# A windowed attention with an MLP on one core: the float16 weighted sums of the last three chunks as two 64-query halves

## The chip, the cores and the metric

One core of one Trainium2 chip runs the kernel. The metric is device time in microseconds (us), from one launch; runs of the kernel before took 605.85, 604.10 and 605.22 us, median 605.22 us.

## The reference, cut to what matters

There are 4 batches, 8 heads, 768 positions and 64 values per head. Each query looks at itself and the 95 positions before it and at 8 global positions; all other scores are set so low that their weight is zero. The result of the attention goes through a two-layer MLP (512 to 2048 to 512) with a smooth activation.

```python
scores = scale * np.matmul(q, k.transpose(0, 1, 3, 2)) + bias      # bias falls with the distance
scores = np.where(keep, scores, -1000000000.0)
a = np.exp(scores - np.max(scores, axis=-1, keepdims=True))
a = a / (np.sum(a, axis=-1, keepdims=True) + 1e-09)
x = np.matmul(a, v)                                                # the weighted sums
h = x @ w_in
out = (h * np.tanh(softplus(h))) @ w_out
```

The change is in `np.matmul(a, v)`.

## The kernel before, in words

**Chunks and blocks.** The 3072 tokens are worked in 12 chunks of 256 queries (`ci` 0 to 11; three for each batch), each of two blocks of 128 queries (`blk`). Of a block's keys only a window is computed: 104 columns (96 earlier positions and 8 global ones) and the block's own 128. The first block of a batch has only its own 128 (`nk` is 1 there, 2 elsewhere; L401).

**Precision.** Chunks 0 to 2 (`CF32 = 3`) work in float32. From chunk 3 on each float32 operand is split into a float16 high part and a float16 low part, and a product is three float16 products: high by high, high by low, low by high.

**Attention, by steps.** A step `t` stands for two heads of one block, 8 steps per chunk; `where` and `shape` (L395 to L404) give its chunk, head group, block and pair of heads.
- `scores` (letter s, L418 to L438) multiplies queries and keys on TensorE, for two steps at a time. Its weights are 64 rows by 64 columns: head `j` uses 64 of the array's rows, each half of 64 queries 64 of its columns, so that four such products stand next to each other in program order.
- `largest` (t) takes the maximum on VectorE, `exps` (y) the exponential on ScalarE, `high_a` and `low_a` (g, p) split the result, and `turn_a` (X) transposes it by a DMA into the tile `AT`: keys on the partitions, 128 queries in the free dimension.
- `weigh` (W, L499 to L522) makes the weighted sums. For chunks 3 and later it takes the loop at L514: for each of two heads `j`, for each window part `kk` and each of the three precision terms, one product with `AT` as the weights (104 or 128 rows by 128 queries) and 64 columns of `v` streamed past them, accumulated in `pav[:, cols]`. That is 12 products a step, 6 in the first block of a batch. In chunks 0 to 2 the loop at L508 is used instead, whose weights are 64 columns of `v`, for two heads in turn.
- `rows` (R, L524) divides by the sums on VectorE, which reads `pav`; high_x, low_x and turn_x (T, U, V) prepare the MLP's input.

**MLP, by steps.** `moe_in` (i, L588, product at L597) makes 24 products of 128 by 128 weights with 256 columns; ScalarE, VectorE and GpSimd compute the activation; `moe_out` (o, L644, product at L656) makes 12 products with 512 columns (in the last chunk some of them with 256 or 128). `checks(1)` (L714) is one product near the end whose weights are 128 rows by 1 column, with 240 columns streamed.

**Order.** Every engine's order is written out by hand in `PROGRAM` (L739 to L796), a list of letters with numbers, and each engine takes its instructions in that order. Chunk 9 begins at step 72. TensorE's order around the steps W72 to W95 is below: each bracket is a run of weighted sums, with the TensorE steps just before and after it. There are 16 such runs.

```
i63 [W73] s78      o62 [W72] i65        i66 [W77 W76] i67   i68 [W75] s82
o67 [W74 W81] s84  s84 [W78 W79] o68    i71 [W82] s86       o71 [W85 W84] i72
i72 [W83 W80] i76  o72 [W87] o73        s92 [W86] i77       o76 [W88] i79
o78 [W89 W91] o79  o79 [W90] i81        o80 [W92 W93] i82   i82 [W94 W95] o81
```

Steps W72, W73, W76 and W77 have 6 products each, the other twenty 12: 264 products in all.

Of the kernel before, what the change touches and what calls it, by code (L numbers as in the profile page):

```python
# [20 lines left out]
P = 128  # L21
# [89 lines left out]
def windowed(st, tc, loc):  # L111


    nc = tc.nc
    L = NS()
    L.__dict__.update(loc)
    B, H, D, S, NB, NCC, NFB = L.B, L.H, L.D, L.S, L.NB, L.NCC, L.NFB
# [283 lines left out]
    def shape(t):  # L401
        ci, g, blk, a2 = where(t)
        first = ci % NCHB == 0 and blk == 0
        return ci, g, blk, a2, first, 1 if first else 2  # L404
# [94 lines left out]
    def weigh(t):  # L499
        ci, g, blk, a2, first, nk = shape(t)  # L500
        AT = pend.pop(t)
        if (ci, blk) not in pavs:
            pavs[ci, blk] = ps.tile([P, DM], F32, name=f"pav{blk}", bufs=1)
        pav = pavs[ci, blk]
        vs = [vown[ci][:, blk]] if nk == 1 else [vcmp[ci][:, blk], vown[ci][:, blk]]
        if ci < CF32:
            pair = slice((g * GH // 2 + a2) * P, (g * GH // 2 + a2 + 1) * P)
            for kk in range(nk):  # L508
                rows_ = slice(0, P if kk == nk - 1 else FB)
                for j in range(2):  # L510
                    h = g * GH + 2 * a2 + j
                    nc.tensor.matmul(pav[j * D:(j + 1) * D, pair], vs[kk][rows_, h * D:(h + 1) * D], AT[rows_, j * nk + kk, :], start=(kk == 0), stop=(kk == nk - 1))  # L512
            return
        for j in range(2):  # L514
            h = g * GH + 2 * a2 + j
            cols = slice(h * D, (h + 1) * D)
            n, last = 0, 3 * nk - 1
            for kk in range(nk):
                rows_ = slice(0, P if kk == nk - 1 else FB)
                for x, y in ((0, 0), (0, 1), (1, 0)):  # L520
                    nc.tensor.matmul(pav[:, cols], AT[rows_, (x * 2 + j) * nk + kk, :], vs[kk][rows_, y, cols], start=(n == 0), stop=(n == last))  # L521
                    n += 1  # L522

    def rows(n):  # L524
# [178 lines left out]
    def checks(i):  # L703
# [26 lines left out]
        "d": lambda p, other=False: low_k(p - 1, other), "N": units, "h": high_v, "l": low_v, "x": window_v,  # L730
        "e": begin, "K": lambda i: masks_far() if i else masks_own(), "L": mask_own, "M": mask_far,
        "s": scores, "t": largest, "y": exps, "g": high_a, "p": low_a, "X": turn_a, "W": weigh,
        "I": identity, "P": turn_p, "F": turned, "O": spread, "m": times_rb,
        "R": rows, "T": high_x, "U": low_x, "V": turn_x,
# [221 lines left out]
```

## Time and profile before

| | before |
|---|---|
| median of three runs | 605.22 us (604.10 to 605.85) |
| the profiled execution's own time | 605.78 us |
| its span, first to last instruction | 604.0 us |
| mean granted TensorE clock | 0.998 of full speed |
| TensorE products (PE) | busy 594.2 us, 98% of the span |
| weight loads (PEld) | busy 412.7 us, 68% |
| ScalarE, VectorE, GpSimd | 75%, 72%, 25% |

How to read the rows further down: PE is TensorE's products, PEld its weight loads, which run beside products. In a shape such as `104*128 104x64 f16` the part with the star is the weights (rows by columns) and the part with the x the streamed operand (rows by columns). L521 is line 521 of the kernel. A row of the timeline gives the start of the first instruction of a group, the time from there to the end of its last, the group, and how many there are. Products are pipelined and their ends are modelled: the duration of one is its latency, longer than the step from one start to the next. So the pace is read from starts, and the start of a group's last product is the row's start plus its length less the mean duration of one. DVE is VectorE, ACT ScalarE, POOL GpSimd.

### The profile page before, as it was taken

What the parts mean: (1) busy time and instruction counts of PE and PEld (TensorE: products, weight loads), DVE (VectorE), ACT (ScalarE), POOL (GpSimd) and SP (SyncE); (2) the same over time, 40 slices, a digit from 0 to 9 for tenths busy, and PEclk for the clock granted to TensorE, in tenths of its full rate; (3) what the DMA queues carried; (4) which work ended last, traced back from release to release, by engine and by line L of the source; (5) the groups of instructions that cost most, each with busy time, mean ns of one, the idle gap of its engine ahead of it and who ended that gap; (6) DMA issues with size and microseconds to landing.
All of it is one profiled execution on the core that took longest, in us unless ns stands there. A gap on an engine that the chain in (4) does not pass through costs nothing.

```text
span 604.0 us, 15002 instructions
## 1 busy us (share of the span) xinstructions
PE 594.2 (98%) x5775; PEld 412.7 (68%) x5775; DVE 437.5 (72%) x1188; ACT 454.2 (75%) x1130; POOL 150.5 (25%) x128
## 2 busy tenths in 40 slices
PE   7999999999999999999999999999999999999996
PEld 3678677785567676767667676767667766766784
DVE  7799989998978795684876767675786766462433
ACT  6899999989978777569676778677876864655652
POOL 0033321331040423123133422141242121301020
PEclk9999999999999999999999999999999999999999
DMA  8998674333294481634454453562345341310001
GB/s 206 274 290 309 218 178 131 102 91 75 76 203 110 66 210 36 162 102 109 69 144 115 131 129 84 162 130 60 101 70 142 68 119 36 89 36 1 35 2 37
DMA packets 123387, 71.14 MB, mean 118 GB/s; under 512 B 91792, under 2 KB 113168, under 8 KB 123312
## 3 DMA queue, kind: packets, MB, share of 16 engines
q1 hardware_dynamic: 122736, 69.88, 45.8%
q8 instruction: 46, 0.75, 0.5%
q10 hardware_dynamic: 576, 0.27, 0.3%
q14 instruction: 29, 0.24, 0.1%
HBM read 38.62 MB, written 6.29 MB: 74 GB/s over the span
## 4 chain that ended last, share of the span: by engine, by line
PE 92%; DMA 4%; ACT 2%; SPq 1%; DVE 0%; issue 0%; ACTq 0%; DVEq 0%
PE ph L597 41%; PE po L656 36%; PE pav L656 4%; PE pav L521 4%; PE sc L437 4%; DMA kr<-kd 2%; DMA vo<-v 2%; PE pav L512 1%; PE ph L490 1%; DMA AT<-hl 1%; PE ph L543 0%; ACT A L460 0%; ACT u L623 0%; ACT AT L148 0%; ACT u L627 0%
## 5 line engine op out<-in xcount | busy, mean ns | idle before, releaser
L597 PE MATMUL ph<-xT,wts 128*128 128x256 f16 x2304 | 263.6, 273 | 0.0
L597 PEld LDWEIGHTS <-wts 128*128 128x128 f16 x2304 | 223.1, 98 | 34.5 <-issue 0.4
L656 PE MATMUL po<-wts,gt 128*128 128x512 f16 (+1 forms) x1056 | 234.4, 374 | 0.0
L656 PEld LDWEIGHTS <-gt 128*128 128x128 f16 x1248 | 115.9, 98 | 118.3
L615 ACT ACTIVATE e<-ph 128x512 f32<-128x512 f32 x90 | 53.2, 591 | 95.5 <-PE ph L597 95.3
L152 POOL TENSOR_TENSOR gt<-gf,gt 128x512 f16<-128x512 f32 x50 | 61.9, 1240 | 229.6 <-DVE gt L146 155.2
L635 DVE CUSTOM_DVE_ANT_0 gf<-gf,u 128x512 f32<-128x512 f32 x96 | 72.3, 756 | 49.6 <-ACT u L627 47.7
L460 ACT ACTIVATE A<-A,nm 128x232 f32<-128x232 f32 (+1 forms) x192 | 88.2, 461 | 12.3 <-DVE nm L451 12.3
L631 DVE SCALAR_TENSOR_TENSOR gf<-e,ph 128x512 f32<-128x512 f32 x90 | 61.0, 682 | 49.1 <-ACT e L615 48.2
L152 POOL TENSOR_TENSOR hl<-A,hl 128x512 f16<-128x512 f32 (+1 forms) x43 | 50.3, 1180 | 110.3 <-ACT hl L148 43.5
L451 DVE CUSTOM_DVE_ANT_0 A<-sc,mb 128x232 f32<-128x232 f32 (+1 forms) x192 | 63.6, 374 | 12.7 <-PE sc L437 12.5
L627 ACT ACTIVATE u<-u 128x512 f32<-128x512 f32 x96 | 59.7, 624 | 1.9
L619 ACT ACTIVATE u<-e 128x512 f32<-128x512 f32 x96 | 59.8, 624 | 1.7
L623 ACT ACTIVATE u<-u 128x512 f32<-128x512 f32 x96 | 59.7, 623 | 1.6
L152 POOL TENSOR_TENSOR wts<-ws,wts 128x512 f16<-128x512 f32 x18 | 22.5, 1255 | 82.0 <-ACT wts L148 75.3
L152 DVE TENSOR_TENSOR gt<-gf,gt 128x512 f16<-128x512 f32 x46 | 34.3, 748 | 6.9 <-ACT gt L148 6.3
L460 ACT ACTIVATION_READ_ACCUMULATOR A<-A,nm 128x1 f32 x192 | 36.2, 188 | 0.0
L521 PEld LDWEIGHTS <-AT 128*128 128x128 f16 (+1 forms) x792 | 29.4, 97 | 7.2 <-DMA AT<-hl 0.8
L148 ACT ACTIVATE gt<-gf 128x512 f16<-128x512 f32 x39 | 24.3, 623 | 11.3 <-DVE gmax L635 9.2
L656 PE MATMUL pav<-wts,gt 128*128 128x512 f16 (+1 forms) x192 | 28.7, 299 | 0.0
L521 PE MATMUL pav<-vo,AT 128*128 128x64 f16 x432 | 28.0, 192 | 0.0
L146 DVE TENSOR_SCALAR gt<-gf 128x512 f16<-128x512 f32 x57 | 25.6, 452 | 1.5
(130 smaller groups left out, 563.8 us busy)
## 6 DMA issues: line engine op xcount, KB each, us to landing
wts<-w_in SPq DMA_DIRECT2D x12, 512.0 KB
wts<-w_out SPq DMA_DIRECT2D x12, 512.0 KB
qr<-qT SPq DMA_DIRECT2D x23, 256.0 KB
kr<-kd SPq DMA_DIRECT2D x32, 184.0 KB
out<-ob SPq DMA_DIRECT2D x23, 256.0 KB
vr<-v SPq DMA_DIRECT2D x9, 512.0 KB
vc<-vo SPq DMA_DIRECT2D x15, 192.0 KB
wr<-w_in SPq DMA_DIRECT2D x4, 512.0 KB
```

The lines of the kernel that those rows point to most:

```text
L152: (nc.vector if other else nc.gpsimd).tensor_tensor(out, in_, high, op=ALU.subtract)
L451: nc.vector.tensor_tensor_reduce(out=A[:, j, 0:w], in0=sc[j][:, 0:w], in1=m, scale=-1.0 / (UNIT if ci < CF32 else UNIT * SQ), scalar=3.0e3 ...
L460: nc.scalar.activation(A[:, j], A[:, j], AF.Exp, bias=nm[:, h:h + 1], scale=-1.0, accum_out=rs[:, h:h + 1])
L521: nc.tensor.matmul(pav[:, cols], AT[rows_, (x * 2 + j) * nk + kk, :], vs[kk][rows_, y, cols], start=(n == 0), stop=(n == last))
L597: nc.tensor.matmul(ph[:, j, :].rearrange("p (b t) -> p b t", b=2), wv4[:, 2 * fb, x, c * P:(c + 1) * P], xT[:, :, y * NCC + c, :], start=( ...
L615: nc.scalar.activation(mish[m]["e"], mish[m]["h"], AF.Exp, scale=-1.0 / (SV * SW), accum_out=esum[:, m:m + 1])
L619: nc.scalar.activation(u, mish[m]["e"], AF.Square, bias=0.5)
L623: nc.scalar.activation(mish[m]["r"], mish[m]["u"], AF.Ln, bias=0.25 / RS, scale=1.0 / RS)
L627: nc.scalar.activation(r, r, AF.Exp, scale=-1.0)
L631: nc.vector.scalar_tensor_tensor(gf, mish[m]["e"], 0.5, mish[m]["h"], op0=ALU.add, op1=ALU.mult)
L635: nc.vector.tensor_tensor_reduce(out=gf, in0=gf, in1=mish[m]["r"], scale=SG / (SV * SW * RS), scalar=0.0, op0=ALU.mult, op1=ALU.max, accum ...
L656: nc.tensor.matmul(pos[ci][t + k][:, cols], gt[:, x, j, t * P:(t + 1) * P], wv4[:, 2 * fb + 1, y, cols], start=(fb == 0 and n == 0), stop= ...
```

## The change

In `weigh`, for chunks 9, 10 and 11, each product with 128 columns of weights becomes two: one on the first 64 queries (columns of the array and partitions of `pav` 0 to 63), one on the other 64. Both stream the same 64 columns of `v`. The halves alternate in the innermost loop, so the two halves of one term follow each other. The start and stop flags of a term are given to both halves. The order of the steps and all else stay.

```diff
@@ -518,7 +518,8 @@
             for kk in range(nk):
                 rows_ = slice(0, P if kk == nk - 1 else FB)
                 for x, y in ((0, 0), (0, 1), (1, 0)):
-                    nc.tensor.matmul(pav[:, cols], AT[rows_, (x * 2 + j) * nk + kk, :], vs[kk][rows_, y, cols], start=(n == 0), stop=(n == last))
+                    for half in (slice(0, D), slice(D, P)) if ci >= 9 else (slice(0, P),):
+                        nc.tensor.matmul(pav[half, cols], AT[rows_, (x * 2 + j) * nk + kk, half], vs[kk][rows_, y, cols], start=(n == 0), stop=(n == last))
                     n += 1
```

## Rows read from the trace of the kernel before

**Rows 1.** The page: busy time by engine, and granted clock in 40 slices.
```profile
PE 594.2 (98%) x5775; PEld 412.7 (68%) x5775; DVE 437.5 (72%) x1188; ACT 454.2 (75%) x1130; POOL 150.5 (25%) x128
...
PEclk9999999999999999999999999999999999999999
```

**Rows 2.** The page: the chain that ended last, by engine and line.
```profile
PE 92%; DMA 4%; ACT 2%; SPq 1%; DVE 0%; issue 0%; ACTq 0%; DVEq 0%
```

**Rows 3.** Busy time in the stretch that holds steps W72 to W95.
```profile
core 0: us, PE busy (x) PEld busy (x) DVE busy (x) ACT busy (x) POOL busy (x), PEclk, DMA share, GB/s
409.00:532.00 123.00, 123.00 (x1243) 86.03 (x1241) 83.65 (x214) 87.10 (x223) 29.49 (x24) 1.00 0.37 86
```

**Rows 4.** Waits of PE over the whole span: total us, times, longest.
```profile
PE ph L318 <- DVE ws L314: 2.7, 1, 2.7
PE pav L512 <- DMA vo<-v: 1.0, 1, 1.0
PE pav L521 <- DMA AT<-hl: 0.3, 1, 0.3
```

**Rows 5.** PE groups by shape from 409 us on: busy us, mean ns of one.
```profile
L521 PE MATMUL pav<-vo,AT 128*128 128x64 f16 x144 | 9.3, 192 | 0.0
L521 PE MATMUL pav<-vc,AT 104*128 104x64 f16 x120 | 8.1, 192 | 0.0
L656 PE MATMUL pav<-wts,gt 128*128 128x128 f16 x96 | 6.7, 219 | 0.0
...
L437 PE MATMUL sc<-wc,ws 64*64 64x168 f16 x216 | 5.7, 237 | 0.0
```

**Rows 6.** Timeline of PE, two runs of 24 weighted-sum products and what follows them.
```profile
523.87 0.25 PE L521 MATMUL pav<-vc,AT 104*128 104x64 f16 x3
...
524.58 2.78 PE L597 MATMUL ph<-xT,wts 128*128 128x256 f16 x24
527.20 0.25 PE L521 MATMUL pav<-vc,AT 104*128 104x64 f16 x3
...
527.91 2.75 PE L656 MATMUL po<-wts,gt 128*128 128x512 f16 x12
```

**Rows 7.** Timeline of PE: weighted sums, the scores of one step, weighted sums.
```profile
447.30 0.25 PE L521 MATMUL pav<-vo,AT 128*128 128x64 f16 x3
447.48 0.63 PE L437 MATMUL sc<-wc,ws 64*64 64x168 f16 x24
448.05 0.26 PE L521 MATMUL pav<-vc,AT 104*128 104x64 f16 x3
448.14 0.25 PE L521 MATMUL pav<-vo,AT 128*128 128x64 f16 x3
```

**Rows 8.** Timeline of PE: float32 products with 64 columns of weights (L543).
```profile
15.56 0.44 PE L490 MATMUL po<-idn,A 128*128 128x128 f32 x2
15.93 1.09 PE L543 MATMUL ph<-idn,ri 128*64 128x128 f32 x16
16.95 0.66 PE L490 MATMUL po<-idn,A 128*128 128x128 f32 x4
```

**Rows 9.** Mean duration of these float32 products over the span.
```profile
L490 PE MATMUL po<-idn,A 128*128 128x128 f32 x56 | 9.7, 289 | 0.5 <-ACT A L460 0.3
...
L543 PE MATMUL ph<-idn,ri 128*64 128x128 f32 x96 | 6.5, 277 | 0.0
```

**Rows 10.** Timeline of PE around the one-column product L714.
```profile
595.15 0.83 PE L656 MATMUL pav<-wts,gt 128*128 128x128 f16 x12
595.92 0.26 PE L714 MATMUL sc<-ind,ones 128*1 128x240 f16 x1
596.11 2.12 PE L656 MATMUL po<-wts,gt 128*128 128x512 f16 x12
```

**Rows 11.** Timeline of PE: the scores of a batch's first block, then weighted sums.
```profile
243.90 0.53 PE L437 MATMUL sc<-wc,ws 64*64 64x64 f16 x24
244.36 0.26 PE L521 MATMUL pav<-vc,AT 104*128 104x64 f16 x3
```

**Rows 12.** The same scores by shape, those begun by 243.95 us: x is the count.
```profile
L437 PE MATMUL sc<-wc,ws 64*64 64x128 f16 x2 | 0.2, 240 | 0.0
L437 PE MATMUL sc<-wc,ws 64*64 64x64 f16 x3 | 0.2, 206 | 0.0
```

**Rows 13.** The same, those begun by 244.045 us.
```profile
L437 PE MATMUL sc<-wc,ws 64*64 64x128 f16 x6 | 0.4, 224 | 0.0
L437 PE MATMUL sc<-wc,ws 64*64 64x64 f16 x9 | 0.3, 197 | 0.0
```

**Rows 14.** Weight loads of the same scores begun by 243.92 us.
```profile
L437 PEld LDWEIGHTS <-ws 64*64 64x64 f16 x4 | 0.1, 103 | 0.2 <-issue 0.2
```

## The prediction, made before the changed kernel ran

> **What bounds the kernel now.** I read the page first. TensorE's products are busy 594.2 us of 604.0, no other engine over 75%, and the granted clock is full in every slice [rows 1]. Busy time alone doesn't prove a bound, so the next view is the chain that ended last: 92% of it is PE [rows 2]. Then the stretch in which the change acts, which the order of steps puts at 409 to 532 us: PE is busy all 123.00 us of it, at full clock, while ScalarE has 87.10 and VectorE 83.65 [rows 3]. The waits of PE confirm it: the only one that ever named the weighted sums is 0.3 us, once in the span, and the longest PE wait anywhere is a start-up one of 2.7 us [rows 4]. So in this stretch, and from there to PE's end, PE has no slack: what the change adds to PE's stream moves the end by as much, and what it saves there would be won in full. The producers of `AT` and the consumer of `pav` (VectorE at L535) have room on both sides; a PE that comes later only gives the first more time.
>
> Then the weighted sums themselves. The groups by shape have 144 and 120 products, 264 in all, as the order of steps says [rows 5]. Their mean of 192 ns is latency; the pace is in the starts. Two runs of 24 take 523.87 to 524.58 and 527.20 to 527.91, 0.71 us each [rows 6], so a product comes every 0.0296 us; the starts are rounded to 0.01, which leaves 0.0292 to 0.0300, and I take 0.0298. All 264 cost 7.9 us now. They stream 64 columns. A 128-column product comes every (0.83 - 0.219) / 11 = 0.0555 us [rows 5, 10], so 64 columns are worth 0.028 us. The pace is thus nearly that of the columns, and a half product still streams all 64 of them. **No column of time is removed**; the best the halves can do is to stand side by side and give the pace of before.
>
> **What is added.** (1) 264 products and 264 weight loads: a term is now two loads of 64 columns and two products. (2) Changes of the weights' width, 128 to 64 columns and back, around each run of weighted sums. (3) Nothing moves: DMAs, order, waits and other engines are the same. The second half's wait for `pav` or `AT` is met when the first's is, so I cost it at nothing; were it not met, PE would show it as a wait, of which there is now 0.3 us in all [rows 4].
>
> **The price of a change of width.** Four places show one.
> - From the weighted sums (128 columns of weights) to the scores (64 by 64): the last of three begins at 447.30 + 0.25 - 0.192 = 447.36, its columns take 0.03, the scores begin at 447.48: a hole of 0.09 us [rows 5, 7].
> - Back: the last score begins at 447.48 + 0.63 - 0.237 = 447.87, its 168 columns take 0.073, the next weighted sum begins at 448.05: 0.10 [rows 5, 7].
> - With all 128 rows in use and only the width changing, in float32: the last of L543 begins at 15.93 + 1.09 - 0.277 = 16.74. A round of its eight takes at most (1.09 - 0.277) / 7 = 0.116, and the next 128-wide one begins at 16.95: 0.09 or a little more [rows 8, 9].
> - In float16 with only the width changing, to a single column and back: the last 128-wide product begins at 595.15 + 0.61 = 595.76 and ends its columns at 595.82; L714 begins at 595.92, and its 240 columns (0.104 us) end at 596.02; the next begins at 596.11. The two holes together are 0.19 us [rows 5, 10].
> By contrast, weighted sums followed by a 128-wide MLP product leave no hole: 524.58 is the 24th step after 523.87 [rows 6]. So a change costs **0.095 us** in either direction, and it goes with the width alone. On top comes a first load that nothing covers. Into 64-wide weights: the first 64-column score begins at 243.90 and the third, the next of its tile, just before 243.95, 0.05 us where a later round takes 0.032 (below): 0.02 more [rows 11, 12]. Into 128-wide ones: the row at 448.05 is 0.26 long where its like is 0.25: 0.01 more [rows 7].
>
> **How many.** Of the 16 runs in the order of steps, 14 are entered from a 128-wide product and 12 left to one: 26 new changes. Two are entered from scores and four left to scores, where a hole stands already; the two entries cost the 0.01 us by which the first load is longer.
> 14 x 0.115 + 12 x 0.105 + 2 x 0.01 = **2.9 us**.
>
> **The pace inside a run.** No row has a float16 pair of column halves over all 128 rows, so I bound it. Below: the pace of before, 0.0298 a pair, since the columns set it. Above: two halves in turn, 2 x 0.0298, 0.06 a pair. The nearest row is the score tile with 64 columns of weights and 64 streamed: three had begun by 243.95, nine by 244.045; six more in two tiles are three rounds in 0.095 us, **0.0317** a round, with the other tiles running beside it [rows 12, 13]. I take 0.0317: 264 - 16 = 248 steps inside runs x 0.0019 = **0.5 us**. Why the halves should overlap: eight pairs of L543 are column halves over all 128 rows and take 0.116 us a pair, no more than the (0.66 - 0.289) / 3 = 0.124 of one full-width float32 product behind it, both with a first load in them [rows 8, 9]. Why the queue should keep up: 24 scores, loads included, begin within 0.53 - 0.22 = 0.31 us, 0.013 a product, where a half needs 0.016 [rows 11, 13].
>
> Here a page speaks against the change more than the rows do. The first four 64-wide loads begin within 0.02 us of each other, and a tile's load and product repeat every 0.0317 us [rows 13, 14]. The Trainium skill ("TensorE: Matmul & The Clock Gate", section "LDWEIGHTS (loading the stationary operand)") puts a load at its columns over 1.2 GHz, an estimate of 0.053 us for 64. By that a pair would take 0.053 and the sum would be 264 x 0.023 = 6.1 us instead of 0.5. The trace's 0.0317 disagrees, and I go by it.
>
> **The sum.** 2.9 + 0.5 = 3.4 us on PE, none of it covered. The profiled execution took 605.78 us (span 604.0 and 1.8 around it), which gives 609.2. That execution is 0.56 above the median of the runs, 605.22; against the median the forecast is **608.6**. About 0.3% of this kernel, 1.8 us, is what a measurement can tell from no change.
>
> **The rivals.**
> - *The halves load in turn.* Both column halves take their weights from the same 128 rows; if their loads queue, a pair takes two rounds of 0.0317, and 264 x (0.0634 - 0.0298) = 8.9 us come on top of 2.9: 617.0. For it: a load nearly fills the round already. Against it: the scores' loads, two of each four on the same 64 rows, start together [rows 14]. Chance 0.05. The load of 0.053 us that the page would have instead gives 605.2 + 2.9 + 6.1 = 614.2, in that case's tail.
> - *TensorE's queue is too slow.* Seven of the runs become 48 products at a stretch. No row shows more than 24 at a pace below 0.02 us. At the old pace a product, a pair takes 0.0596: 7.9 + 2.9 = 10.8, 616.0. Chance 0.04.
> - *Not slower: no hole between 128-wide and half-wide weights.* If TensorE emptied only where the rows change too, or for float32, the 26 holes would be absent. What is left is the pace and 14 first loads: 0.5 + 0.3 = 0.8 us, 606.0, no measurable change. It decides at the first MLP product behind a run: begins at once, or 0.1 us later. For it: L543 is float32 and L714 has one column, not 64. Against it: between them both doubts are met, and the hole was the same in all. Chance 0.06.
> - *Faster.* The pace would have to fall under that of the streamed columns, which no row shows; I leave 0.01 for it. That the change doesn't act can't be: the slices are explicit.
>
> **How the numbers follow.** The forecast has 0.84. Its own bounds: 26 x 0.09 with no first load and the old pace is 2.3, 607.5; holes and loads of 0.125 and a pace 0.005 slower are 3.3 + 1.2 = 4.5, 609.7. The runs shown scatter by 0.6 above and 1.1 below their median; a median scatters less, and I allow 0.6 to 0.7 on either side: 606.9 to 610.4. It leaves out the two slow rivals and the two others, 0.16. Slower by over 0.3%: 0.84 + 0.05 + 0.04 = 0.93. Within: 0.06. Faster: 0.01.
>
> **What would show it.** Right: 528 products at L521 with 64 columns of weights from chunk 9 on; a hole of about 0.1 us on either side of a run, as between i65 and W72; both halves of a term starting some ns apart, pairs 0.032 us apart, so that a run of 24 pairs takes 0.76 us where it took 0.71; the stretch from step i63 to o83 longer by 3.4 us, all else on PE as before; a clock still at full. Wrong: a pair every 0.05 us or more (loads or queue in turn), or MLP products that follow at once (no hole); a new wait of PE for `AT` or `gt`, or a clock that falls between the holes, would be causes not named here.

## The result and the profile after

The changed kernel took 609.08 us (median of four runs, 608.51 to 609.34) against 605.17 us for the kernel before (four runs, 604.10 to 605.85): a ratio of 1.0065, 95% interval 1.0051 to 1.0079. It is slower by 3.9 us; the forecast was 3.4 us more, 608.6.

The two profiled executions can be compared without the scatter of whole runs. The order of steps puts everything that the change touches between the first product of step i63 and the first of step o81, and TensorE never rests there. That stretch took 527.91 - 409.74 = 118.17 us before and 530.53 - 409.00 = 121.53 us after: **3.36 us**. From the start of o81 to the start of TensorE's last product it is 70.77 us before and 70.78 after. Ahead of the stretch, where the two programs are the same, i63 came 0.74 us earlier in the execution of after; behind TensorE's last product that execution took 0.6 us longer. These are the scatter that a whole run carries.

The busy time of the changed kernel's engines over just this stretch (columns as in [rows 3]):

```profile
core 0: us, PE busy (x) PEld busy (x) DVE busy (x) ACT busy (x) POOL busy (x), PEclk, DMA share, GB/s
...
408.99:530.53 121.54, 121.54 (x1478) 83.52 (x1476) 80.92 (x206) 83.13 (x217) 29.48 (x24) 1.00 0.37 86
```

PE is still busy all the time and at full clock; VectorE and ScalarE still have about 40 us to spare. A hole of 0.1 us doesn't show in this busy time, because each product is listed with a latency of 0.19 us or more that reaches across the hole; holes are read from starts. The groups of PE by shape, from 409 us on, against [rows 5]:

```profile
L522 PE MATMUL pav<-vo,AT 128*64 128x64 f16 x288 | 9.9, 196 | 0.0
L522 PE MATMUL pav<-vc,AT 104*64 104x64 f16 x240 | 8.8, 198 | 0.0
```

These are the 528 products with 64 columns of weights, twice 264. Now the timeline of PE around the last two runs, W92 W93 and W94 W95, to be laid beside [rows 6]:

```profile
523.36 2.75 PE L657 MATMUL po<-wts,gt 128*128 128x512 f16 x12
526.04 0.28 PE L522 MATMUL pav<-vc,AT 104*64 104x64 f16 x6
526.16 0.26 PE L522 MATMUL pav<-vo,AT 128*64 128x64 f16 x6
526.25 0.26 PE L522 MATMUL pav<-vc,AT 104*64 104x64 f16 x6
...
526.73 0.26 PE L522 MATMUL pav<-vo,AT 128*64 128x64 f16 x6
526.92 2.79 PE L598 MATMUL ph<-xT,wts 128*128 128x256 f16 x24
529.65 0.28 PE L522 MATMUL pav<-vc,AT 104*64 104x64 f16 x6
...
530.33 0.26 PE L522 MATMUL pav<-vo,AT 128*64 128x64 f16 x6
530.53 2.76 PE L657 MATMUL po<-wts,gt 128*128 128x512 f16 x12
```

All terms of the sum can be read here.
- **The hole on the way in.** The last of the twelve L657 products begins at 523.36 + 2.75 - 0.38 = 525.73, its 512 columns end at 525.95, the first half begins at 526.04: 0.09 us. Before, a weighted sum followed an MLP product without a hole: 527.20 is the 24th step after 524.58 [rows 6].
- **The first load.** The first row of a run lasts 526.04 to 526.16, 0.12 us for three terms, the later ones 0.095: 0.02 us that nothing covers.
- **The pace.** From 526.16 to 526.73 there are 18 terms: 0.0317 us for a pair of halves. A row of six products stands where one of three stood, and takes 0.095 instead of 0.089 us.
- **The hole on the way out.** The last row's three terms end at 526.73 + 0.095 = 526.82, the MLP begins at 526.92: 0.10 us. The MLP's own row is 2.79 long instead of 2.78, which the forecast puts down to a first load of 128 columns that nothing covers. The starts of the other runs show the same: 0.09 to 0.10 us at every one of the 26 new places.

One thing here goes beyond the forecast. Where a run lies beside scores, both sides now have weights of 64 columns, and only the rows differ (128 or 104 against 64). The timeline of PE after, a run that is left to scores and the next, which is entered from them:

```profile
447.48 0.26 PE L522 MATMUL pav<-vo,AT 128*64 128x64 f16 x6
447.67 0.63 PE L437 MATMUL sc<-wc,ws 64*64 64x168 f16 x24
448.23 0.28 PE L522 MATMUL pav<-vc,AT 104*64 104x64 f16 x6
```

The three terms of the first row end at 447.48 + 0.095 = 447.575, and the scores begin at 447.67: 0.095 us. The last score begins at 447.67 + 0.63 - 0.237 = 448.06, its columns end at 448.14, and the next run begins at 448.23: 0.09 us. So a change of the rows from 128 or 104 to 64, or back, makes the same hole with the width unchanged. The alternation of 104 and 128 rows inside a run makes none.

PE's waits show nothing new in the stretch (rows to be laid beside [rows 4], and one that is new; total us, times, longest):

```profile
PE ph L318 <- DVE ws L314: 2.7, 1, 2.7
PE pav L512 <- DMA vo<-v: 1.6, 1, 1.6
PE pav L522 <- DMA AT<-hl: 0.4, 1, 0.4
...
PE ph L598 <- DMA xT<-xhl: 0.3, 1, 0.3
```

Against [rows 4], the wait for a transposed tile is 0.4 us instead of 0.3, still once in the span. The new one is a wait of the MLP for its input. Both end ahead of the stretch, at 388 and 223 us, where the two programs are the same.

### The profile page after: what moved, and what is told of

Same layout as the page of the kernel before. It is cut to its first block, busy times and chain, and to the rows that moved or that the text cites. A ratio compares the mean times of both kernels' runs of the same rounds, so it can differ in the third digit from the quotient of the medians.

```text
span 607.2 us, 15530 instructions
## 1 busy us (share of the span) xinstructions
PE 596.1 (98%) x6039; PEld 412.4 (68%) x6039; DVE 437.9 (72%) x1188; ACT 454.1 (75%) x1130; POOL 150.6 (25%) x128
## 4 chain that ended last, share of the span: by engine, by line
PE 92%; DMA 4%; DVE 1%; ACT 1%; SPq 1%; issue 0%; DVEq 0%; ACTq 0%
PE ph L598 40%; PE po L657 35%; PE pav L657 4%; PE sc L437 4%; PE pav L522 4%; PE pav L512 2%; DMA vo<-v 1%; PE po L490 1%; PE ph L544 1%; DMA vc<-vo 1%; DMA xT<-xhl 1%; PE ph L490 1%; DMA AT<-hl 1%; DMA kr<-kd 1%; DVE A L451 0%
## 5 line engine op out<-in xcount | busy, mean ns | idle before, releaser
L657 PE MATMUL po<-wts,gt 128*128 128x512 f16 (+1 forms) x1056 | 234.4, 375 | 0.0
L657 PEld LDWEIGHTS <-gt 128*128 128x128 f16 x1248 | 115.7, 98 | 118.5 <-POOL gt L152 0.2
L522 PEld LDWEIGHTS <-AT 128*128 128x128 f16 (+3 forms) x1056 | 29.1, 104 | 9.9 <-issue 4.7
L657 PE MATMUL pav<-wts,gt 128*128 128x512 f16 (+1 forms) x192 | 28.7, 299 | 0.0
L522 PE MATMUL pav<-vo,AT 128*128 128x64 f16 (+1 forms) x576 | 28.6, 194 | 0.0
```

What stands on the lines that cost most here:

```text
L522: nc.tensor.matmul(pav[half, cols], AT[rows_, (x * 2 + j) * nk + kk, half], vs[kk][rows_, y, cols], start=(n == 0), stop=(n == last))
L657: nc.tensor.matmul(pos[ci][t + k][:, cols], gt[:, x, j, t * P:(t + 1) * P], wv4[:, 2 * fb + 1, y, cols], start=(fb == 0 and n == 0), stop= ...
```

## The experiments

The same measure serves for all: the stretch from the first product of i63 to the first of o81, from the starts of the two rows in the timeline of PE.

| run | i63 | o81 | stretch | time, us (runs) |
|---|---|---|---|---|
| before | 409.74 | 527.91 | 118.17 | 605.17 (4) |
| after | 409.00 | 530.53 | 121.53 | 609.08 (4) |
| x0, after again | 408.34 | 529.86 | 121.53 | 608.95 (5) |
| x1, one term of each run | 408.77 | 529.81 | 121.05 | 608.08 (1) |
| x2, halves one after the other | 410.52 | 533.19 | 122.67 | 610.80 (4) |
| x3, quarters | 408.54 | 531.11 | 122.58 | 609.00 (1) |
| x4, after with fewer runs | 410.98 | 531.37 | 120.39 | 608.33 (10) |
| x5, before with the same moves | 408.53 | 526.72 | 118.19 | 605.59 (10) |
| x6, halves from chunk 3 on | 415.43 | 536.95 | 121.52 | 615.15 (4) |
| x7, before with wide ones | 408.49 | 527.02 | 118.53 | 604.99 (1) |

The ratios of x0 and x2 are to 605.00 us for the kernel before (nine runs on one chip), those of x4 to x6 to 605.57 us (19 runs on another chip).

Theory: 26 holes and their first loads cost 2.9 us, the slower pace 0.5, and TensorE has no slack to cover either. Rivals: the cost goes with the number of products and loads; the halves would queue; the moves or the rest of the kernel take part.

**x1: the holes without the halves.** Only one term of each run is split.

```diff
+                    lone = (t in (78, 86) and j == 0 and n == 0) or (t in (72, 73, 75, 76, 80, 81, 82, 84, 87, 88, 90, 91, 93, 95) and j == 1 and n == last)
-                    for half in (slice(0, D), slice(D, P)) if ci >= 9 else (slice(0, P),):
+                    for half in (slice(0, D), slice(D, P)) if lone else (slice(0, P),):
```

> One term alone of each of the 16 runs is split into halves (the last term of a run, the first term in the two runs that are entered from scores); the other 248 products stay 128 queries wide. That makes 16 products more instead of 264, but the same 26 new changes of width. If the holes at the changes carry the cost (my theory): the stretch from step i63 to step o81 is longer than before by 14 x 0.115 + 12 x 0.105 = 2.9 us and about nothing for the pace, so 121.0 to 121.2 us where before had 118.17 and the change 121.53. If the cost goes with the number of products and loads: 16/264 of 3.4, 0.2 us, so about 118.4.

Measured: 121.05 us, 2.88 more than before. The timeline of PE in x1, a run that is left to scores and the next, which is entered from them:

```profile
446.93 0.25 PE L523 MATMUL pav<-vc,AT 104*128 104x64 f16 x3
447.02 0.37 PE L523 MATMUL pav<-vo,AT 128*128 128x64 f16 x4
447.32 0.63 PE L437 MATMUL sc<-wc,ws 64*64 64x168 f16 x24
447.88 0.38 PE L523 MATMUL pav<-vc,AT 104*64 104x64 f16 x4
448.10 0.25 PE L523 MATMUL pav<-vo,AT 128*128 128x64 f16 x3
```

The row at 447.02 has four products and lasts 0.37 us instead of 0.25: its last term comes as two halves, and there is a hole ahead of them, in the middle of a run, with the same tile and 128 rows of weights on both sides, and no wait. In the run behind the scores the hole follows the first term: from 447.88 to 448.10 it is 0.22 us for three terms that took 0.09 [rows 7]. Sixteen products more cost 86% of what 264 cost. What is left of the change is 121.53 - 121.05 = 0.48 us, the pace.

**x2: must the halves alternate?** All terms of one half come ahead of all terms of the other.

```diff
-            n, last = 0, 3 * nk - 1
-            for kk in range(nk):
...
+            last = 3 * nk - 1
+            for half in (slice(0, D), slice(D, P)) if ci >= 9 else (slice(0, P),):
+                n = 0
+                for kk in range(nk):
...
```

> Of each head, all terms of the first 64 queries come first and then all terms of the second 64, so that neighbours in the queue use the same half of the array, but for one seam in each group. Same 528 products, same 26 changes. If the halves overlap only because they alternate: each product then takes its own round of about 0.0317 us, 264 x (0.0634 - 0.0298) = 8.9 us come on top of the 2.9 us of the holes, less some 0.03 us for each of the seams where the two halves still meet (48 within the groups and some between them, 1.5 us or more), so the stretch from i63 to o81 is 127 to 130 us and the time 614 to 617 us. If the queue lets the second half pass the first: 121.5 us and about 609 us, as with the change.

Measured: 122.67 us and 610.80 us, ratio 1.0091 (1.0068 to 1.0114). My first alternative, 127 to 130 us, is wrong: the halves overlap nearly as well as with the change. The timeline of PE in x2 shows how, in a run of 24 terms (the list in between goes on in the same way):

```profile
473.77 0.31 PE L523 MATMUL pav<-vc,AT 104*64 104x64 f16 x4
473.89 0.20 PE L523 MATMUL pav<-vo,AT 128*64 128x64 f16 x1
473.92 0.20 PE L523 MATMUL pav<-vc,AT 104*64 104x64 f16 x1
473.93 0.19 PE L523 MATMUL pav<-vo,AT 128*64 128x64 f16 x1
473.95 0.20 PE L523 MATMUL pav<-vc,AT 104*64 104x64 f16 x1
...
474.52 0.29 PE L523 MATMUL pav<-vo,AT 128*64 128x64 f16 x4
474.74 0.28 PE L599 MATMUL ph<-xT,wts 128*128 128x256 f16 x1
```

In program order a head has three products with `vc` and three with `vo` on the first half, and only then three with `vc` on the second. Here `vc` already comes a fourth time ahead of the first `vo`, and from then on they take turns. The trace doesn't name the half, but by the program a fourth product with `vc` is the second half's: its products begin while the first half's still stand ahead of them in the program. So a product here waited for those on its own columns of the array, not for the other half. What x2 loses is the start and the end of a run, where one half works alone: 474.74 - 473.77 = 0.97 us where the change takes 526.92 - 526.04 = 0.88. Over 16 runs the stretch shows 1.14 us, 0.07 a run.

**x3: is the pace the load's?** Four quarters of 32 queries.

```diff
-                    for half in (slice(0, D), slice(D, P)) if ci >= 9 else (slice(0, P),):
+                    for half in [slice(i * 32, i * 32 + 32) for i in range(4)] if ci >= 9 else (slice(0, P),):
```

> Four quarters of 32 queries in turn in place of two halves of 64: 1056 products with loads of 32 columns. If the 0.0317 us of a pair of halves is the load of 64 columns that the 64 streamed columns don't quite cover: a load of 32 takes half, the pace falls to that of the streamed columns, 0.029 to 0.030 us for four quarters, and the stretch from i63 to o81 is 120.9 to 121.2 us (holes alone). If each load and product costs a step of its own in the queue: four quarters take longer than two halves, by up to the double, 0.032 to 0.063 us a term, and the stretch is 121.6 to 130 us.

Measured: 122.58 us, in the range of the second alternative; but 1.0 us of it are two stalls that neither had (below). Within a run both are seen, one after the other, as this one of 24 terms in the timeline of PE in x3 shows (12 products a row, three terms):

```profile
447.75 0.27 PE L522 MATMUL pav<-vc,AT 104*32 104x64 f16 x12
447.85 0.26 PE L522 MATMUL pav<-vo,AT 128*32 128x64 f16 x12
447.94 0.27 PE L522 MATMUL pav<-vc,AT 104*32 104x64 f16 x12
448.02 0.28 PE L522 MATMUL pav<-vo,AT 128*32 128x64 f16 x12
448.11 0.29 PE L522 MATMUL pav<-vc,AT 104*32 104x64 f16 x12
448.21 0.29 PE L522 MATMUL pav<-vo,AT 128*32 128x64 f16 x12
448.31 0.32 PE L522 MATMUL pav<-vc,AT 104*32 104x64 f16 x12
448.44 0.29 PE L522 MATMUL pav<-vo,AT 128*32 128x64 f16 x12
448.66 0.39 PE L657 MATMUL po<-wts,gt 128*128 128x512 f16 x1
```

From 447.85 to 448.11 three terms take 0.087 us, 0.029 a term: the streamed columns alone, as the load of 32 would have it. From 448.11 on, after 48 products, a row takes 0.10, and once 0.13: 0.033 us and more for four products with their loads, some 8 ns for each product. So a second limit shows behind the first: from there on TensorE starts no more than one load and product every 8 ns. In the last run it goes further (timeline of PE in x3, idle time and what ended it in brackets; "issue" is a wait for nothing that the profile shows):

```profile
530.24 0.20 PE L522 MATMUL pav<-vc,AT 104*32 104x64 f16 x1
530.64 0.27 PE L522 MATMUL pav<-vc,AT 104*32 104x64 f16 x11 [0.20 <-issue]
```

Here 0.37 us pass between two products beyond the ordinary step. The waits of PE have one more of this kind in the stretch, listed with 0.5 us: between two MLP products, 1.3 us behind the run above, where the next product begins at 450.82, 0.64 us after the columns of the one ahead of it. Together these 1.01 us are about the 1.05 us by which x3 is over the change. What TensorE waited for in these two is open. Halves ask for a product every 0.016 us and stay clear of it: the run at 529.65 of the change, 48 products long, keeps 0.095 us a row to its end.

**x4 and x5: fewer changes, same products.** In x4 the steps W73, W74, W81, W84, W85, W87, W89, W91, W92, W93 and the division R22 come later in the order, each just ahead of the next run; x5 has the same order with the kernel before. The diff shows TensorE's steps of the order alone, and of them the pieces that change, three to a line.

```diff
-i63 W73 s78 o62 W72 i65        o67 W74 W81 s84 W78 W79 o68    o71 W85 W84 i72 W83 W80 i76
+i63 s78 o62 W73 W72 i65        o67 s84 W74 W81 W78 W79 o68    o71 i72 W85 W84 W83 W80 i76
-o72 W87 o73 o74 s92 W86 i77    W89 W91 o79 W90 i81            o80 W92 W93 i82 W94 W95 o81
+o72 o73 o74 s92 W87 W86 i77    o79 W89 W91 W90 i81            o80 i82 W92 W93 W94 W95 o81
```

> The changed kernel with ten of its steps of weighted sums (and one division on VectorE behind two of them) later in the order, so that 16 runs become 10: 8 entered from and 8 left to 128-wide products, 16 new changes of width instead of 26; 528 products as before. If the cost goes with the changes: 8 x 0.115 + 8 x 0.105 + 2 x 0.01 + 254 x 0.0019 = 2.3 us, so the stretch from i63 to o81 is 120.4 us (118.17 before, 121.53 with the change) and the time about 1.1 us under the change's. If it goes with the number of products: 121.5 us, the change's time. Should TensorE wait for a transposed tile or a division comes too late, the profile shows it as a wait of PE.

> The kernel before with the same eleven moves, as a control: its weighted sums are as wide as the MLP's products, so the number of runs costs nothing except that two runs no longer lie beside scores, where a change stands either way. Theory: the stretch from i63 to o81 is 118.1 to 118.3 us, the time within 0.3% of before. If the moves themselves cost or bring something (a wait of PE, a later division), it shows here, and the run with both is read against this one.

Measured: x4 120.39 us and ratio 1.0038 (1.0027 to 1.0048); x5 118.19 us and ratio 0.9999 (0.9987 to 1.0011). The moves alone do nothing; with the halves, ten changes less are worth 121.53 - 120.39 = 1.14 us, 0.114 each. The times agree: x4 is 608.33 - 605.57 = 2.76 us over the kernel before of its own set, the change 3.91 and 3.95 over that of its two sets, so 1.15 to 1.19 less.

**x6: three times as much.** `ci >= 3` in place of `ci >= 9`.

> The halves in all nine float16 chunks instead of the last three: 792 products split, 50 runs, of which 39 are entered from and 38 left to 128-wide products, 77 new changes of width, and 11 entries from scores. If holes and pace add up as in the last three chunks and nothing covers them: 39 x 0.115 + 38 x 0.105 + 11 x 0.01 + 742 x 0.0019 = 10.0 us, so 615.2 us (614.5 to 616). If TensorE has slack in chunks 3 to 8 that takes them: less, down to the change's 608.5 to 609.

Measured: 615.15 us, ratio 1.0149 (1.0128 to 1.0170). The last three chunks take 121.52 us as with the change, and step i63 comes late: from i16 to i63 it is 415.43 - 85.88 = 329.55 us where before had 409.74 - 87.03 = 322.71. The 6.84 us are the other six chunks' share; 10.0 - 3.4 = 6.6 were expected. There is no slack in them either.

**x7: a hole taken away from the kernel before.** The weights of L714 become 128 columns wide; their other result rows are unused.

```diff
-    ones = cp.tile([P, 1], F16, name="ones")
+    ones = cp.tile([P, P], F16, name="ones")
...
-            nc.tensor.matmul(votes[0], ones, ind, start=True, stop=True)
+            nc.tensor.matmul(every, ones, ind, start=True, stop=True)
```

> The kernel before, with the weights of the one-column product near the end (the column of ones that sums the flags) made 128 columns wide; its other 127 result rows are not used. If a hole comes from the change of width alone, both of its holes of 0.095 us go: from the start of the last o81 product group on, TensorE's last product comes 70.58 us later where before had 70.77, and the step from the product ahead of it to the product behind it shrinks from 0.35 to 0.16 us. If the hole has another cause (the wait of that product for VectorE's flags, its own kind of operands), it stays: 70.77. The time moves by less than the scatter either way.

Measured, timeline of PE in x7, against [rows 10]:

```profile
594.26 0.83 PE L656 MATMUL pav<-wts,gt 128*128 128x128 f16 x12
594.93 0.27 PE L715 MATMUL sc<-ind,ones 128*128 128x240 f16 x1
595.03 2.11 PE L656 MATMUL po<-wts,gt 128*128 128x512 f16 x12
```

From the first of the twelve to the one-off product it is 0.67 us where it was 0.77, and from there to the next 0.10 where it was 0.19: both holes are gone, and from o81 to the last product it is 70.58 us instead of 70.77. So neither the wait for VectorE nor the operands made them. The time, 604.99 us in one run, can't show so little. This execution also waited 0.3 us for a transposed tile ahead of W92, which makes up nearly all by which its stretch of 118.53 us is longer than that of before.

**x0: the change again.**

> The changed kernel again, in more rounds, to narrow the interval. By the trace the stretch from step i63 to o81 grew by 3.36 us and what follows it on TensorE by 0.01; the medians differ by 3.9. If the 0.5 us between them is scatter of the start and of the last store (theory): 3.0 to 3.8 us. If it is a cost outside that stretch: 3.9 again, with a second part of the timeline that is longer in each profile.

Measured: 608.95 us (five runs) against 605.00 (nine runs), ratio 1.0069 (1.0049 to 1.0088), and again a stretch of 121.53 us with 70.79 behind it. The theory's 3.0 to 3.8 us was not met by the median, which is 3.9 again; no second part of the timeline is longer either. Against the 605.57 us of the other chip's 19 runs it would be 3.4 to 3.5, but a comparison from one chip to another is weak. In the profiles of the table up to x5 the program ahead of i63 is the same, and i63 came between 408.34 and 410.98 us. From the start of o81 to the end of the span the ten profiles take 76.1 to 76.7 us, and kernels with and without halves lie at both ends (x3 76.1 and after 76.7, before 76.1 and x5 76.6). The intervals hold 3.4, so scatter is enough to explain the 0.5 us, but it is not shown that there is nothing else in it.

## Why the prediction was right

- **TensorE has no slack there.** Shown: the stretch grew by what was added, nothing behind it changed, and x6 repeats it over all float16 chunks.
- **26 changes at 0.095 us and their first loads, 2.9 us.** Shown by x1 (2.88 us, with 16 products more in place of 264) and, change by change, by x4 against the change, with x5 as the control (0.114 each). That a change of width makes a hole by itself, with 104 and with 128 rows of weights and without a wait, is shown by x7 and by the hole in the middle of x1's runs. "It goes with the width alone" is too narrow: after the change, the six holes beside scores stand between weights of the same width, with 64 rows on one side. The sum is untouched by this, as it counted no new hole there.
- **The pace, 0.0317 us a pair, 0.5 us.** Measured 0.0317; what the change has above x1 is 0.48. That the score tile, with half the rows, would give the same figure was an assumption that held; no run shows why it had to. The Trainium skill ("TensorE: Matmul & The Clock Gate", section "LDWEIGHTS (loading the stationary operand)") gives an estimate of 0.053 us for a load of 64 columns; it did not come, as pairs with their loads repeat every 0.0317 us in this trace. What sets the 0.0317 is not settled. x3 fits a bound by the load: with loads of half the size a term falls to 0.029. But the kernel before has one load of 128 columns for every product [rows 1] and still a step of 0.0298, so the time of a load doesn't go with its columns alone.
- **The sum, 3.4 us.** 3.36 in the stretch. In it is one small thing that the forecast didn't have. Before, step o72 begins about 0.12 us after the columns of the last product of i76 have ended, without a change of width (timeline of PE before):

```profile
478.62 2.79 PE L597 MATMUL ph<-xT,wts 128*128 128x256 f16 x24
481.37 2.75 PE L656 MATMUL po<-wts,gt 128*128 128x512 f16 x12
```

From one start to the other it is 2.75 us; after, it is 482.29 - 479.66 = 2.63. The stall is there in all three profiles of kernels without split sums (0.13 us in x5, 0.14 in x7) and in none of the seven with them, x1 included; why is open. Without it the stretch would have grown by 3.48 us with the change and by 3.0 with x1: the term for the holes is 0.1 too small, and the stall, of which the forecast knew nothing, makes up for it. That part of the agreement is luck.
- **The waits.** The prediction calls 0.3 us the only wait of PE that ever named the weighted sums; [rows 4] has another, 1.0 us at L512, the float32 weighted sums of the first chunks. It lies ahead of the stretch and changes nothing in the sum.
- **The rivals.** Loads in turn: no, the halves run side by side, in whatever order they come. A queue that is too slow: not at 0.016 us a product, but x3 meets a limit at about half of that. No hole with half-wide weights: it is there at every one of the 26 places.
- The time came out 0.5 us above the forecast of 608.6, inside the range; those 0.5 us are not explained by the mechanism (x0).

## What to carry to other kernels

On a TensorE that never rests, count the changes of the weights' shape in program order before you narrow a product: here each change of width costs 0.11 us, and so, nearly, does one between 64 rows and 104 or 128. A product that is split by queries saves no streamed column to pay for it. If narrow products are needed, put them together in as few runs as their buffers allow, or give them the width of their neighbours (x4, x7). The pace was forecast here from a tile of the same width with the same streamed columns elsewhere in the trace; that is one case.

## What the runs showed that I had not expected

In x2 products on different columns of the array didn't begin in program order: the second half's first product begins ahead of three of the first half's that are earlier in the program. And in x3, after 48 products with quarters, TensorE started no more than one load and product every 8 ns, and twice it stood still for 0.4 to 0.6 us with nothing in the profile to wait for. A hole also stands where only the rows of the weights change, between 104 or 128 and 64.
